# First block of a convolution and SiLU kernel: two weight units loaded ahead, first taps and some rounding moved from VectorE to ScalarE

## The chip, the cores and the metric

One core of a Trainium2 chip. The time is device microseconds of one execution of the whole program. Repeated executions of one kernel agree within some tenths of a per cent; all runs told of here are in the fast state, at a mean granted TensorE clock (the share of full speed that the throttle allowed) of 0.992 to 0.998. "VectorE", "ScalarE", "GpSimd", "SyncE" and "TensorE" are the engines; the profile calls them DVE, ACT, POOL, SP and PE, and PEld is TensorE's weight load.

## The reference

```python
# x: (8, 4096, 192); weight: (8 heads, 7 taps); w_in: (192, 2048); w_out: (2048, 192), all float32
w   = softmax(weight, axis=-1)                       # per head
y   = causal depthwise convolution of x over the sequence, 7 taps, 24 channels a head
h   = y.reshape(32768, 192) @ w_in
g   = h * sigmoid(h)                                 # SiLU
out = g @ w_out
```

The weights arrive as 64-bit floats. The kernel reads them as pairs of 32-bit words and makes float32 of them on the chip; this is the "rounding" below.

## The kernel before

The tokens are done in 32 blocks of 1024. In block 0 the plain products are computed while weights are still being made ready; blocks 1 to 31 use a scheme with fewer products that needs combined weights, and repeat a fixed plan. The change concerns block 0 and the first taps of block 1.

Each of the four units of w_in, and then of w_out, is loaded raw and rounded. A `shared` rounding gives two of its ten instructions to ScalarE; they stand in the middle, with VectorE's instructions before and behind them. Before the change the first two units of w_in are rounded so, and none of w_out:

```python
class Pinned: ...                        # keeps an engine's instructions in the program's order
vec = Pinned(nc.vector)

def rounded(dst, words, shared):         # shortened
    vec.tensor_single_scalar(ex, hi, 0x7FF * one, op=ALU.bitwise_and)
    vec.tensor_single_scalar(st, lo, 0xFF, op=ALU.bitwise_and)
    vec.tensor_scalar(ex, ex, ..., op0=ALU.max, op1=ALU.min)
    if shared:
        nc.scalar.sign(st, st)           # not pinned
        nc.scalar.activation(ex, ex, AF.Copy, bias=..., scale=8.0)
    else:
        vec.tensor_single_scalar(st, st, 1, op=ALU.min)
        vec.tensor_scalar(ex, ex, ..., op0=ALU.subtract, op1=ALU.mult)
    ...                                  # five more on VectorE; the second needs st, the fourth ex
```

The evictions of block 0 (the reads that empty TensorE's result banks) are Silu instructions on ScalarE, each of which frees one of the 8 accumulation banks. The scheduler that compiles the program may put what is not pinned in another order:

```python
def up_plain(b, j):                      # shortened: unit j, 8 banks, 24 matmuls (48 in the trace)
    hs = {(a, n, e): bank() for a, n in outs for e in range(2)}
    ...
            for e in range(2):
                nc.scalar.activation(g[:, n, e, :], hs[a, n, e], AF.Silu)

def conv(b, k, i):                       # shortened: tap i of channel third k
    if i == 0:
        pin(nc.vector.tensor_scalar(dst, src, scalar1=tap, scalar2=None, op0=ALU.mult))
    else:
        pin(nc.vector.scalar_tensor_tensor(out=dst, in0=src, scalar=tap, in1=dst, ...))

for k in range(NK):                      # head of block 0
    turn_in(0, k)                        # transpose, waits for a third of x
    for i in range(K):
        conv(0, k, i)
    spread(0, k)                         # copies to both partition halves ("dup"), SyncE's queue
    round_in(0, k)
load_in(2, nc.sync)
round_in(1)
load_in(3, nc.sync)
for j in range(NJ):                      # NJ = 4
    up_plain(0, j)
    round_in(j + 2) or round_out(j + 2 - NJ)   # and the load of w_out unit j
for j in range(2, NJ):
    round_out(j)
...                                      # transposes and taps of block 1, then down_plain(0), block 1, ...
```

Of the kernel before, what the change touches and what calls it, by code (L numbers as in the profile page):

```python
# [10 lines left out]
I32 = mybir.dt.int32  # L11
AF = mybir.ActivationFunctionType
# [5 lines left out]
def kernel(  # L18
# [24 lines left out]
    nc = tc.nc  # L43
# [3 lines left out]
    H, K = weight.shape  # L47
    NT = B * S
    DFF = moe_w_in.shape[1]
    P = 128  # L50
    R = 64
    NK = D // R
    grp = D // H
    pad = K - 1
    TB = 512
# [4 lines left out]
    NJ = NM // 2  # L60
# [10 lines left out]
    tpool = ctx.enter_context(tc.tile_pool(name="tp", bufs=3))  # L71
    gpool = ctx.enter_context(tc.tile_pool(name="gp", bufs=2 * NJ))
# [30 lines left out]
    def pin(ins):  # L103
        return tc.keep_in_program_order(ins)
# [15 lines left out]
    def load(b, ks=range(NK)):  # L120
        if b not in nats:
            nats[b] = xpool.tile([P, NK, TB // SQ, SQ], F32, tag="nat", name="nat")
        nat = nats[b]
        for k in ks:
            for i in range(P // SQ):
                c = R * k + SQ * (i % 2)
                (nc.sync if b or k or i % 2 else nc.scalar).dma_start(  # L127
                    out=nat[SQ * i : SQ * i + SQ, k, :, :],
                    in_=x_v[2 * b + i // 2][:, :, c : c + SQ],
                )  # L130
# [22 lines left out]
    WC = 2 * NK * P  # L153
# [6 lines left out]
    raws = {}  # L160

    def raw_tile(key):
        raws[key] = tpool.tile([P, 4 * TB], I32, tag="t", name="raw")[:, 0 : 2 * WC]
        return raws[key]

    def load_in(j, queue):
        raw = raw_tile(("i", j)).rearrange("p (a k c) -> p a k c", a=2, k=NK)
        for e in range(2):
            for a in range(2):
                c = 2 * P * (NM * a + 2 * j + e)  # L170
                queue.dma_start(
                    out=raw[R * e : R * e + R, a, :, :], in_=in32[:, :, c : c + 2 * P]
                )

    def load_out(q, queue):
        raw = raw_tile(("o", q)).rearrange("p (a e d) -> p a e d", a=2, e=2)
        for a in range(2):
            queue.dma_start(out=raw[:, a, :, :], in_=out32[a, q])
# [48 lines left out]
    def round_in(j, k=None):  # L227

        words = raws["i", j].rearrange("p (a k c t) -> p a k c t", a=2, k=NK, t=2)
        if k is None:  # L230
            rounded(
                wr[j].rearrange("p a k c -> p a (k c)"),
                words.rearrange("p a k c t -> p a (k c) t"),
                j < 2,
            )
        else:
            rounded(wr[j][:, :, k, :], words[:, :, k], j < 2)
        if k in (None, NK - 1):

            del raws["i", j]  # L240
            for e in range(2):
                nc.gpsimd.dma_start(
                    out=ws[j][R * e : R * e + R], in_=wr[j][R - R * e : 2 * R - R * e]
                )

    def round_out(q):
        rounded(
            wo[q].rearrange("p a e d -> p a (e d)"),
            raws.pop(("o", q)).rearrange("p (a x t) -> p a x t", a=2, t=2),
            False,  # L250
        )

    def comb(out, u, v, op):
# [24 lines left out]
        comb(a_(1, 0), a_(0, 0), a_(1, 0), ALU.subtract)  # L278

    load_in(0, nc.sync)  # L280
    load(0, (1, 2))
    load_in(1, nc.sync)


    hot = const.tile([P, NK, H], F32, name="hot")
# [38 lines left out]
    def turn_in(b, k):  # L324
        if k == 0 and b:
            xt = xts[b] = xpool.tile([P, NK, pad + TB], F32, tag="xt", name="xt")
            if b * TT % S == 0:
                nc.gpsimd.memset(xt[0:R, :, 0:pad], 0.0)
            else:
                nc.gpsimd.tensor_copy(xt[0:R, :, 0:pad], tails.pop(b))  # L330
        xt = xts[b]
        pin(
            nc.vector.transpose(  # L333
                xt[:, k, pad : pad + TB], nats[b][:, k, :, :].rearrange("p k c -> p (k c)")
            )
        )
        if k == NK - 1:
            if b:
                nc.sync.dma_start(out=xt[R:P, :, 0:pad], in_=xt[0:R, :, TB : TB + pad])
            if (b + 1) * TT % S:  # L340
                tails[b + 1] = xpool.tile([R, NK, pad], F32, tag="tail", name="tail", bufs=2)
                nc.sync.dma_start(out=tails[b + 1], in_=xt[R:P, :, TB : TB + pad])

    def conv(b, k, i):

        src = xts[b][:, k, i : i + TB]
        dst = nats[b][:, k, :, :].rearrange("p k c -> p (k c)")
        tap = taps[:, k, i : i + 1]
        if i == 0:
            pin(nc.vector.tensor_scalar(dst, src, scalar1=tap, scalar2=None, op0=ALU.mult))  # L350
        else:
            pin(
                nc.vector.scalar_tensor_tensor(  # L353
                    out=dst, in0=src, scalar=tap, in1=dst, op0=ALU.mult, op1=ALU.add
                )
            )

    def spread(b, k):

        if k == 0:  # L360
            dups[b] = xpool.tile([P, 2, NK, TB], F32, tag="dup", name="dup")
        src = nats[b][:, k, :, :].rearrange("p k c -> p (k c)")
        for n in range(2):
            for e in range(2):
                nc.sync.dma_start(
                    out=dups[b][R * e : R * e + R, n, k, :], in_=src[R * n : R * n + R, :]
                )
# [255 lines left out]
    def step(b, token):  # L623

        if token[0] == "-":
            b, token = b - 1, token[1:]
        name, arg = token.split(".") if "." in token else ("", "")
        if b < 0 or b >= NB or not name or (b, token) in did:
            return
        did.add((b, token))  # L630
        digits = [int(c) for c in arg]
        if name[0] in "PE":
            product(b, digits[0], name)
        elif name[0] in "sCg":
            if b:
                sums_h(b, name, digits[0])
        elif name == "t":
            sum_g(b, *digits)
        elif name[0] in "Mzyx":
            merge(b, name)  # L640
        elif name == "o":
            turn_out(b, *digits)
        elif b + 1 < NB:
            {"i": turn_in, "v": conv, "w": win}[name](b + 1, *digits)
            if name == "v" and digits[1] == K - 1 and (b, "down") in did:
                spread(b + 1, digits[0])
                if digits[0] == NK - 1 and b + 2 < NB:
                    load(b + 2)
# [11 lines left out]


    for k in range(NK):
        turn_in(0, k)
        for i in range(K):
            conv(0, k, i)
        spread(0, k)
        round_in(0, k)
    load_in(2, nc.sync)
    round_in(1)
    load_in(3, nc.sync)  # L670
    for j in range(NJ):
        up_plain(0, j)
        if j + 2 < NJ:
            round_in(j + 2)
            load_out(j, nc.sync)
        else:
            round_out(j + 2 - NJ)
            load_out(j, nc.sync)
        if j == 1:
            load(1)  # L680
    for j in range(2, NJ):
        round_out(j)
# [59 lines left out]
```

## Time and profile before

| part of the run before | from the trace |
|---|---|
| time, median (3 runs) | 2425.77 us (2425.73 to 2425.81) |
| span of the profiled run | 2424.1 us |
| TensorE's solid run begins with unit 2 (index 1) at | 38.20 us |
| the four units of block 0 are through at | 69.37 us |
| down products of block 0 | 41.35 us |
| up products of block 1, and of a settled block | 39.73 us, 37.97 us |

These are lines of the timeline of ScalarE in the kernel before: start, busy time, line, operation, output and input, count, and in brackets the idle time before and what ended it.

```profile
66.80 1.09 ACT L413 ACTIVATE g<-ps 128x512 f32<-128x512 f32 x2 [1.49 <-PE ps L403]
69.37 1.09 ACT L413 ACTIVATE g<-ps 128x512 f32<-128x512 f32 x2 [1.49 <-PE ps L403]
109.08 0.58 ACT L560 COPY cmb<-ps 128x512 f32<-128x512 f32 x1 [38.62 <-PE ps L547]
```

The reader is to see two things. The evictions come in twos, each released by TensorE: ScalarE keeps up and waits. And after the last one it has nothing at all to do for 38.62 us.

### The profile page before, as it was taken

What the parts mean: (1) busy time and instruction counts of PE and PEld (TensorE: products, weight loads), DVE (VectorE), ACT (ScalarE), POOL (GpSimd) and SP (SyncE); (2) the same over time, 40 slices, a digit from 0 to 9 for tenths busy, and PEclk for the clock granted to TensorE, in tenths of its full rate; (3) what the DMA queues carried; (4) which work ended last, traced back from release to release, by engine and by line L of the source; (5) the groups of instructions that cost most, each with busy time, mean ns of one, the idle gap of its engine ahead of it and who ended that gap; (6) DMA issues with size and microseconds to landing.
All of it is one profiled execution on the core that took longest, in us unless ns stands there. A gap on an engine that the chain in (4) does not pass through costs nothing.

```text
span 2424.1 us, 43022 instructions
## 1 busy us (share of the span) xinstructions
PE 2389.0 (99%) x17744; PEld 944.2 (39%) x17744; DVE 2076.5 (86%) x2827; ACT 981.7 (40%) x1845; POOL 66.4 (3%) x100
## 2 busy tenths in 40 slices
PE   6999999999999999999999999999999999999998
PEld 3344433334433334333444333443334443334432
DVE  8988888898888888888988889888889888898875
ACT  3134533345433345333454333553334543335432
POOL 3300000000000000000000000000000000000000
PEclk9999999999999999999999999999999999999999
DMA  7321222222222212221222222122222222221220
GB/s 151 73 52 32 44 44 53 41 43 40 36 53 50 43 32 42 47 53 40 41 41 39 53 48 46 31 39 50 53 40 40 38 43 53 46 43 36 36 40 14
DMA packets 452005, 111.65 MB, mean 46 GB/s; under 512 B 421792, under 2 KB 426912, under 8 KB 451808
## 3 DMA queue, kind: packets, MB, share of 16 engines
q1 hardware_dynamic: 447888, 106.63, 23.6%
q8 instruction: 139, 2.28, 0.4%
q0 software_dynamic: 608, 1.84, 0.4%
q10 hardware_dynamic: 3312, 0.42, 0.1%
q14 instruction: 58, 0.48, 0.1%
HBM read 31.49 MB, written 25.17 MB: 23 GB/s over the span
## 4 chain that ended last, share of the span: by engine, by line
PE 98%; DVE 1%; DMA 0%; SPq 0%; ACT 0%; issue 0%; POOL 0%; ACTq 0%; POOLq 0%; DVEq 0%
PE ps L439 49%; PE ps L496 46%; PE ps L547 2%; PE ps L403 1%; DVE nat L353 0%; DVE two L111 0%; SPq L127 0%; DMA nat<-in_x_dram 0%; DVE cmb L598 0%; DMA raw<-in_moe_w_in_dram 0%; DVE mh L111 0%; DVE wr L111 0%; DVE xt L333 0%; POOL out_dram L615 0%; DVE osb L608 0%
## 5 line engine op out<-in xcount | busy, mean ns | idle before, releaser
L439 PE MATMUL ps<-dup,ws 64*128 64x512 f32 x2480 | 869.1, 589 | 0.0
L496 PE MATMUL ps<-g,wo 128*32 128x512 f32 x2976 | 662.0, 593 | 0.0
L463 DVE TENSOR_TENSOR g<-u,ps 128x512 f32<-128x512 f32 x744 | 485.6, 680 | 117.6 <-PE ps L439 88.8
L439 PE MATMUL ps<-win,wr 64*128 64x512 f32 x1488 | 568.8, 589 | 0.1
L496 PE MATMUL ps<-t,wo 128*32 128x512 f32 (+1 forms) x4464 | 500.7, 450 | 0.0
L460 ACT ACTIVATE g<-g 128x512 f32<-128x512 f32 x744 | 444.7, 631 | 99.9 <-DVE g L463 99.9
L439 PEld LDWEIGHTS ps<-dup,ws 64*128 64x128 f32 x2480 | 363.8, 187 | 289.5 <-issue 273.8
L496 PE MATMUL ps<-t,wx 128*32 128x512 f32 x2976 | 453.0, 592 | 0.0
L353 DVE SCALAR_TENSOR_TENSOR nat<-xt,taps,nat 128x512 f32<-128x512 f32 x576 | 432.0, 750 | 15.1
L439 PE MATMUL ps<-dup,wr 64*128 64x512 f32 x992 | 419.3, 596 | 0.0
L454 ACT COPY u<-ps 128x512 f32<-128x512 f32 x496 | 277.5, 588 | 228.7 <-PE ps L439 225.8
L586 ACT COPY cmb<-ps 96x512 f32<-96x512 f32 x31 | 18.0, 581 | 832.2 <-PE ps L496 832.2
L480 DVE TENSOR_TENSOR t<-g 128x1024 f32<-128x1024 f32 x248 | 299.8, 1220 | 26.7 <-PE ps L496 26.7
L480 DVE TENSOR_TENSOR t<-g,t 128x1024 f32<-128x1024 f32 x248 | 303.4, 1224 | 18.3 <-PE ps L496 7.4
L439 PEld LDWEIGHTS ps<-win,wr 64*128 64x128 f32 x1488 | 234.0, 187 | 174.6 <-issue 145.7
L496 PEld LDWEIGHTS ps<-t,wo 128*32 128x32 f32 x4464 | 178.3, 110 | 222.6 <-issue 205.2
L439 PE MATMUL ps<-win,ws 64*128 64x512 f32 x496 | 241.5, 589 | 0.0
L496 PE MATMUL ps<-g,wx 128*32 128x512 f32 x1488 | 234.7, 592 | 0.0
L496 PEld LDWEIGHTS ps<-t,wx 128*32 128x32 f32 x2976 | 121.9, 110 | 278.2 <-issue 268.7
L598 DVE TENSOR_TENSOR cmb<-cmb,ps 96x512 f32<-96x512 f32 x155 | 105.7, 682 | 141.9 <-ACT u L583 139.7
L439 PEld LDWEIGHTS ps<-dup,wr 64*128 64x128 f32 x992 | 160.8, 187 | 127.2 <-issue 112.0
L496 PEld LDWEIGHTS ps<-g,wo 128*32 128x32 f32 x2976 | 168.5, 110 | 97.7 <-issue 97.7
(56 smaller groups left out, 1194.6 us busy)
## 6 DMA issues: line engine op xcount, KB each, us to landing
dup<-nat SPq DMA_DIRECT2D x384, 128.0 KB, 2.3
nat<-in_x_dram SPq DMA_DIRECT2D x382, 64.0 KB, 2.4
out_dram<-osb SPq DMA_DIRECT2D x376, 64.0 KB, 2.0
raw<-in_moe_w_in_dram SPq DMA_DIRECT2D x16, 192.0 KB, 4.8
raw<-in_moe_w_out_dram SPq DMA_DIRECT2D x8, 384.0 KB, 3.6
ws<-wr POOLq DMA_DIRECT2D x8, 192.0 KB, 4.4
xt<-xt SPq DMA_DIRECT2D x31, 4.5 KB, 1.9
tail<-xt SPq DMA_DIRECT2D x24, 4.5 KB, 1.9
```

The costliest lines, as they stand in the source:

```text
L353: nc.vector.scalar_tensor_tensor(out=dst, in0=src, scalar=tap, in1=dst, op0=ALU.mult, op1=ALU.add)
L403: nc.tensor.matmul(hs[a, n, e], rows(wr[j], e)[:, a, k, :], rows(d, e)[:, n, k, :], start=k == 0, stop=k == NK - 1,)
L439: nc.tensor.matmul(bk[b, m, bn], rows(w, half), rows(v, half), start=first, stop=True, skip_group_check=True,)
L454: pin(copy(u, bk[b, m, "1"]))
L460: pin(nc.scalar.activation(g, g, AF.Silu))
L463: pin(nc.vector.tensor_tensor(g, us.pop((b, m, i)), bk[b, m, bn], op=ALU.add))
L480: pin(nc.vector.tensor_tensor(t[i // 2][:, i % 2, :], u, v, op=ALU.subtract))
L496: nc.tensor.matmul(accs[b][i][SQ * q : SQ * q + SQ, cols], lhs[:, e, SQ * c : SQ * c + SQ], rhs[:, e, cols] if i < 5 else rhs[:, e, ts(q, ...
L547: nc.tensor.matmul(acc[k][R * n : R * n + R, :], wo[j][:, a, e, R * k : R * k + R], gs[b, j, a][:, n, e, :], start=j == 0 and a == 0 and e ...
L586: pin(nc.scalar.copy(c[0], acc[0][0:n, :]))
L598: pin(nc.vector.tensor_tensor(out_, u, v, op=ALU.add))
```

## The change

The intent: take the wait for unit 3's weights away by loading units 3 and 4 ahead into tiles that the Silu results will use later, take three first taps and part of the last roundings off VectorE, which is the chain of the first 38 us, and unit 2's load off SyncE's queue.

```diff
     def raw_tile(key):
-        raws[key] = tpool.tile([P, 4 * TB], I32, tag="t", name="raw")[:, 0 : 2 * WC]
+        pool, tag = (gpool, "g") if key in (("i", 2), ("i", 3)) else (tpool, "t")
+        raws[key] = pool.tile([P, 4 * TB], I32, tag=tag, name="raw")[:, 0 : 2 * WC]
 ...
     def round_out(q):
         rounded(..., 
-            False,
+            q >= NJ // 2,
         )
 ...
     load_in(0, nc.sync)
+    load_in(1, nc.gpsimd)
     load(0, (1, 2))
-    load_in(1, nc.sync)
 ...
-        if i == 0:
+        if i == 0 and b < 2:
+            pin(nc.scalar.activation(dst, src, AF.Copy, scale=tap))
+        elif i == 0:
             pin(nc.vector.tensor_scalar(dst, src, scalar1=tap, scalar2=None, op0=ALU.mult))
 ...
     for k in range(NK):
-        turn_in(0, k)
-        for i in range(K):
+        if k == 0:
+            turn_in(0, 0)
+            conv(0, 0, 0)
+        for i in range(1, K):
             conv(0, k, i)
         spread(0, k)
+        if k == 0:
+            load_in(2, nc.sync)
+            load_in(3, nc.sync)
+        if k < NK - 1:
+            turn_in(0, k + 1)
+            conv(0, k + 1, 0)
         round_in(0, k)
-    load_in(2, nc.sync)
     round_in(1)
-    load_in(3, nc.sync)
```

Units are counted from 0 in the code and from 1 in the text, as in the prediction: its "unit 3" is index 2. Blocks are counted from 0 in both.

## The prediction

> **What bounds the kernel now.** I began with the busy table of the page: one engine is busy for the whole span, so only idle time of that engine can be won.
>
> ```profile
> PE 2389.0 (99%) x17744; PEld 944.2 (39%) x17744; DVE 2076.5 (86%) x2827; ACT 981.7 (40%) x1845; POOL 66.4 (3%) x100
> ```
>
> The span is 2424.1 us, so TensorE lacks 35 us in all. Next came the chain of waits in order of time, to see where they lie (start, duration, what).
>
> ```profile
> 37.09 0.97 DVE wr L111
> 38.06 0.14 issue
> 38.20 31.17 PE ps L403 x144
> 69.37 41.35 PE ps L547 x192
> 110.72 20.47 PE ps L439 x88
> 131.19 0.10 issue
> 131.30 19.15 PE ps L439 x88
> 150.45 36.22 PE ps L496 x384
> 186.67 37.97 PE ps L439 x176
> ```
>
> From 38.20 us on, the chain is TensorE alone until the last merge at 2408 us. A settled block takes 36.22 + 37.97 us, 0.216 us per up matmul. Block 1 took 20.47 + 0.10 + 19.15 = 39.73 us for the same 176 matmuls: **1.76 us are lost at the passage from block 0 to block 1**. Everything else that can move lies ahead of 38.20 us. The change touches nothing in the settled loop but the first tap of block 1, so its worth is: the move of 38.20, plus what it returns of the 1.76 us, and no more.
>
> Ahead of 38.20 us the chain is VectorE. Its timeline (start, busy, line, operation, count, idle before) has no gap from the first transpose to the end of the second unit's rounding:
>
> ```profile
> 6.01 0.57 DVE L111 TENSOR_TENSOR each<-wexp,hot 128x56 f32<-128x56 f32 x3
> 6.61 0.33 DVE L111 TENSOR_REDUCE taps<-each 128x21 f32<-128x168 f32 x1
> 6.86 0.70 DVE L333 STREAM_TRANSPOSE xt<-nat 128x512 f32<-128x512 f32 x1
> 7.60 0.49 DVE L350 TENSOR_SCALAR nat<-xt,taps 128x512 f32<-128x512 f32 x1
> 8.12 4.69 DVE L353 SCALAR_TENSOR_TENSOR nat<-xt,taps,nat 128x512 f32<-128x512 f32 x6
> 12.72 0.49 DVE L111 TENSOR_SCALAR two<-raw 128x256 int32<-128x256 int32 x2
> ...
> 37.09 0.96 DVE L111 SCALAR_TENSOR_TENSOR wr<-mh,two 128x768 f32<-128x768 f32 x1
> 40.62 1.33 DVE L111 TENSOR_SCALAR two<-raw 128x768 int32<-128x768 int32 x2 [2.57 <-DMA raw<-in_moe_w_in_dram]
> ```
>
> The reader is to see three groups of transpose, seven taps and a rounding of 8.43 us each (6.86 to 15.29, to 23.74, to 32.29), then 5.77 us of rounding, and only then, at 40.62, the wait for unit 3 that the change aims at.
>
> **What the skill says.** "ScalarE: Activation LUTs", What ACT_TABLE_LOAD costs, gives 186 ns + 0.833 ns per element and some 93 ns for each pointer operand; for 512 elements with a tap as pointer 706 ns. The trace has 631 ns for a 512-element Silu from SBUF to SBUF, where the formula without pointer gives 613: it agrees. The same page, Table sets, says that cheap functions are in every set (it does not name sign). The trace has one table load at 2.39 us, and sign and copy run under it until the Silu's load at 34.95; I expect no third load. "DMA: Bandwidth & Descriptors", Issuing engines are not separate DMA queues: transfers from all queues interleave on the same 16 engines, so a second queue saves only issue time. In the trace those engines are 90% busy and more from 4 to 10 us, at some 140 to 200 GB/s. "TensorE: Matmul & The Clock Gate", Part 1, has half speed after an idle window of about 3.4 us. Here TensorE idles 3.91 us before 32.31 us, and its weight loads then come every 0.43 us instead of 0.215: it agrees.
>
> **The change, part by part.**
> (a) Units 3 and 4 ahead. This takes away the 2.57 us at 40.62. On TensorE's path it is worth nothing directly: unit 2's 48 matmuls take 48 x 0.2155 = 10.3 us from 38.20, to 48.5; the late rounding of unit 3 ended at 47.9 already. VectorE is only earlier afterwards.
> (b) First taps of block 0 on ScalarE. VectorE drops three instructions of 0.52 us start to start, 1.55 us. In return group 0 waits for the tap in series, 0.71 + 0.05 us of handing over = 0.76. For the two others ScalarE works beside the rounding, but the sign of that rounding queues behind it: it starts at 0.74 instead of 0.52 us into the rounding, which holds the OR that needs it back by about 0.2 us. Sum: 1.55 - 0.76 - 0.4 = **0.4 us gained**.
> (c) Unit 2's load through GpSimd, put ahead of the head mask in the program. GpSimd's timeline:
>
> ```profile
> 1.40 2.10 POOL L143 DMA_DIRECT2D xt<-in_x_dram  x3 [0.47 <-issue]
> 3.48 0.14 POOL L286 MEMSET hot<- 128x24 f32 x1
> 3.70 1.05 POOL L290 TENSOR_SCALAR_AFFINE_SELECT hot<-hot 64x24 f32<-64x24 f32 x4
> ```
>
> An issue there occupies the engine: 0.70 us each here, 0.55 to 0.70 for the later swaps. Four more, at an estimated 0.6 to 0.8 us, are 2.4 to 3.2 us, so the mask that was ready at 4.75 us comes at 7.2 to 8.0. VectorE needs it at 6.01 for its tap table: **1.2 to 2.0 us lost, on the path**, for both the transpose and the taps stand behind that table. The same 0.79 MB now also shares the engines with unit 1's weights and the second third of x. Those were all in by about 12 us; 0.79 MB more at some 185 GB/s is 4 us of transfer, some of it after them. I put the second third at 14 to 15 us. The new order wants it for a transpose before the rounding, at 8.5 + 6.2 = 14.7 us, where the old one first rounded and asked at 15.3. That may cost 0 to 1 us, say 0.4.
> (d) Rounding of the last two w_out units shared with ScalarE. It drops two VectorE instructions of about 0.8 us for each unit, some 1.6 us each against the old 8 us; ScalarE has nothing to do from 70.5 to 109 us. First taps of block 1: another 1 us or so. With (a) VectorE reaches block 1 some 5 us sooner. What that returns is read where TensorE's loads wait at the passage:
>
> ```profile
> 113.14 0.38 PEld L439 LDWEIGHTS ps<-dup,ws 64*128 64x128 f32 x4 [0.48 <-DMA dup<-nat]
> 120.72 0.29 PEld L439 LDWEIGHTS ps<-dup,ws 64*128 64x128 f32 x2 [0.42 <-DVE g L463]
> 130.07 0.29 PEld L439 LDWEIGHTS ps<-win,ws 64*128 64x128 f32 x2 [0.47 <-DVE g L463]
> ```
>
> All of them wait for VectorE or for a copy that VectorE's convolution released late, so I count on **1.5 of the 1.76 us**.
> Sum: + 1.6 (mask, middle) + 0.4 (x) - 0.4 (taps) - 1.5 (passage) = + 0.1 us. I allow that the scheduler may set part of GpSimd's issues behind the mask, or that they run faster than the old ones, and take 0.7 us off: 2425.77 + 0.1 - 0.7, about **2425.1 us**.
>
> **The rivals.**
> First, the plain reading of the intent: 2.57 us of wait, 1.5 of taps and 1.76 at the passage all come off the end, 2420. For it speaks that each wait is there in the trace; against it, that the first lies beside TensorE's work with 0.6 us to spare, and that one tap in three stays in series.
> Second, GpSimd or the transfers become the bound of the start: four slow issues (1 us each) put the mask at 8.8 us, a loss of 2.8, and x arrives 1 to 2 us late on top; with little returned at the passage that is 2428. For it speaks the full transfer time from 4 to 10 us; against it, that the early mask has 1.26 us of slack.
> Third, the first copies of block 0 to both halves (dup) fall behind 1.57 MB of units 3 and 4 on the same queue. At 200 GB/s these take 8 us. In the old run the first copies landed at 18.9 us and TensorE then waited anyway, so a landing at 25 still leaves 24 + 24 matmuls room before 38 us, and with less idling before the last third, so at full clock. I expect no loss, or one below 1 us.
> Fourth, ScalarE becomes a bound at 70 to 90 us: 0.85 + 0.83 us for each of two units in 38 idle us; no.
>
> **Range and chances.** The start may move by -0.6 (mask and x both in time) to +3 us, the passage returns 0.8 to 1.76 us. The ends are 2423.4 or 2422.4 with an earlier start than I can explain, and 2428.0; since both ends at once are rare, I take 2422.4 to 2427.8. Two per cent are 48.5 us; all that lies ahead of the solid TensorE work is 38.2 us, and only 7 us of matmul-free waiting stands after. So faster 0.01, slower 0.01, same 0.98.
>
> **What would show it.** In the timeline of the changed kernel: the mask's select on GpSimd after the four issues, ending at 7 to 8 us, and the tap table on VectorE waiting for it; the first tap on ScalarE at 0.7 us; an idle stretch of VectorE before the second transpose, released by x, of 0 to 1 us; TensorE's solid run beginning at 38.5 to 40 us instead of 38.20; no wait for unit 3 or 4; block 1's up matmuls in 38.0 to 38.9 us instead of 39.73; settled blocks at 74.19 us as before. The prediction is wrong downward if the mask is not held up, since then the start is at 37.7; and upward if x comes much later than 15 us, if TensorE waits for dup at 30 us, or if the settled blocks change.

## The result

The changed kernel took **2454.17 us** (median of 4 runs, 2453.81 to 2454.35) against 2425.79 us (4 runs of the kernel before, beside it): 28.4 us longer, a ratio of 1.0116 with a 95% interval of 1.0101 to 1.0131. The ratios here are taken over fast runs; they aren't quite the ratios of the medians. That is inside the 2% that were called "same", but far outside the range of 2422.4 to 2427.8.

First the chain of waits of the changed kernel after 78 us (start, duration, what). L407 is the up products of block 0, L551 its down products, L443 and L500 those of later blocks.

```profile
94.67 5.34 PE ps L407 x12
100.02 41.35 PE ps L551 x192
141.37 37.97 PE ps L443 x176
179.33 36.22 PE ps L500 x384
```

Block 0's four units are through at 100.02 us instead of 69.37. From there on nothing is slower: the down products take 41.35 us as before, and block 1's up products take 37.97 us, so the 1.76 us of the passage are all returned. The account at the end of block 1's up products: start 40.92 - 38.20 = +2.72, units 59.10 - 31.17 = +27.93, passage -1.76, in all +28.89 us. Of the span's +28.6 this leaves 0.3 us, which is gained behind the last product. So one stretch, 41 to 100 us, holds the whole loss. TensorE's timeline there:

```profile
40.92 20.87 PE L407 MATMUL ps<-dup,wr 64*128 64x512 f32 x96 [1.49 <-ACT g L417]
77.49 5.40 PE L407 MATMUL ps<-dup,wr 64*128 64x512 f32 x12 [15.70 <-ACT g L417]
84.28 5.90 PE L407 MATMUL ps<-dup,wr 64*128 64x512 f32 x24 [1.39 <-ACT g L417]
94.67 5.34 PE L407 MATMUL ps<-dup,wr 64*128 64x512 f32 x12 [4.49 <-ACT g L417]
```

Units 2 and 3 run through (96 matmuls), then TensorE waits three times, and each time what ends the wait is L417, a Silu eviction. The last unit's 48 matmuls come in pieces of 12, 24 and 12 and take from 61.8 to 100.0 us. The waits are 15.70 + 1.39 + 4.49 = 21.58 of the 27.93 us. The other 6.35 us come with them: the 48 matmuls take 16.65 us instead of 10.30, and the granted clock is 0.50 from 77 to 81 us and again from 95 to 99 us, behind the two long waits. Why are evictions late on an engine that had 38 idle us? The timeline of ScalarE (L203 and L204 are the shared rounding's sign and copy, L352 the first taps):

```profile
75.24 0.84 ACT L203 ACTIVATE two<-two 128x768 int32<-128x768 int32 x1 [22.66 <-DVE two L111]
76.11 0.84 ACT L204 ACTIVATE two<-two 128x768 int32<-128x768 int32 x1
76.86 1.07 ACT L417 ACTIVATE g<-ps 128x512 f32<-128x512 f32 x2
82.03 0.84 ACT L203 ACTIVATE two<-two 128x768 int32<-128x768 int32 x1 [4.11 <-DVE two L111]
82.89 0.84 ACT L204 ACTIVATE two<-two 128x768 int32<-128x768 int32 x1
83.64 2.04 ACT L417 ACTIVATE g<-ps 128x512 f32<-128x512 f32 x4
92.19 1.95 ACT L352 ACTIVATE nat<-xt,taps 128x512 f32<-128x512 f32 x3 [6.51 <-POOL wr L256]
94.05 3.98 ACT L417 ACTIVATE g<-ps 128x512 f32<-128x512 f32 x8
```

ScalarE is idle for 22.66 us while the eight banks of unit 3 fill (all are full when TensorE stops at 61.79 us), because the next instruction in its queue is the sign of the rounding of w_out's unit 3, and that needs VectorE. VectorE comes to that rounding at 73.79 us:

```profile
73.79 1.42 DVE L111 TENSOR_SCALAR two<-raw 128x768 int32<-128x768 int32 x2
80.58 1.42 DVE L111 TENSOR_SCALAR two<-raw 128x768 int32<-128x768 int32 x2
```

73.79 + 1.42 = 75.21, and the sign starts at 75.24; 80.58 + 1.42 = 82.00, and the second sign starts at 82.03. The order is no accident of the run: it is in the compiled queue. Runs of equal instructions of ScalarE after the table load, as compiled (the traces show the same order):

```
before:   32 Silu | 3 copies of block 0's results | ...
changed:  16 Silu | sign, copy | 2 Silu | sign, copy | 4 Silu | 3 taps of block 1 | 10 Silu | 3 copies | ...
```

The Trainium skill, "TensorE: Matmul & The Clock Gate", Part 1 (engine queue depths), says in one clause that ScalarE and VectorE are strict FIFO. The trace agrees: 22.66 us without overtaking. The wait before the taps is put down to a GpSimd instruction (L256) that was not its input. The profile names the one that came last by its inference; the taps needed block 1's transposes and the copy of its history behind them, issued at 89.79 us with a median of 1.9 us to landing. In e1, below, that copy is named.

The head, for comparison with the prediction's part (c). From the timelines of GpSimd and VectorE, changed kernel:

```profile
3.87 2.47 POOL L173 DMA_DIRECT2D raw<-in_moe_w_in_dram  x4
6.33 0.78 POOL L292 TENSOR_SCALAR_AFFINE_SELECT hot<-hot 64x24 f32<-64x24 f32 x3
7.15 0.57 DVE L111 TENSOR_TENSOR each<-wexp,hot 128x56 f32<-128x56 f32 x3 [0.94 <-POOL hot L292]
9.54 4.69 DVE L357 SCALAR_TENSOR_TENSOR nat<-xt,taps,nat 128x512 f32<-128x512 f32 x6 [0.84 <-ACT nat L352]
16.32 0.71 DVE L335 STREAM_TRANSPOSE xt<-nat 128x512 f32<-128x512 f32 x1 [2.09 <-DMA nat<-in_x_dram]
```

The four issues hold GpSimd for 2.47 us, the mask behind them (`hot`, which channel belongs to which head) makes VectorE wait 0.94 us, the serial first tap 0.84 us, and the second third of x another 2.09 us.

### The profile page after: what moved, and what is told of

Its sections match the earlier page's. It is cut to its first block, busy times and chain, and to the rows that moved or that the text cites. A ratio compares the mean times of both kernels' runs of the same rounds, so it can differ in the third digit from the quotient of the medians.

```text
span 2452.7 us, 43043 instructions
## 1 busy us (share of the span) xinstructions
PE 2394.2 (98%) x17744; PEld 940.7 (38%) x17744; DVE 2070.5 (84%) x2817; ACT 989.2 (40%) x1855; POOL 69.7 (3%) x104
## 3 DMA queue, kind: packets, MB, share of 16 engines
q8 instruction: 139, 2.28, 0.4%
## 4 chain that ended last, share of the span: by engine, by line
PE 96%; DVE 2%; SPq 1%; issue 0%; DMA 0%; ACT 0%; POOL 0%; ACTq 0%; POOLq 0%; DVEq 0%
PE ps L443 48%; PE ps L500 46%; PE ps L551 2%; DVE two L111 1%; DVE mh L111 0%; SPq L127 0%; PE ps L407 0%; DMA nat<-in_x_dram 0%; DVE cmb L602 0%; DVE nat L357 0%; DMA raw<-in_moe_w_in_dram 0%; SPq L369 0%; DVE wo L111 0%; ACT nat L352 0%; ACT g L417 0%
## 5 line engine op out<-in xcount | busy, mean ns | idle before, releaser
L443 PE MATMUL ps<-dup,ws 64*128 64x512 f32 x2480 | 869.9, 589 | 0.0
L500 PE MATMUL ps<-g,wo 128*32 128x512 f32 x2976 | 662.0, 593 | 0.0
L443 PE MATMUL ps<-win,wr 64*128 64x512 f32 x1488 | 567.7, 589 | 0.0
L500 PE MATMUL ps<-t,wo 128*32 128x512 f32 (+1 forms) x4464 | 500.7, 450 | 0.0
L443 PEld LDWEIGHTS ps<-dup,ws 64*128 64x128 f32 x2480 | 363.0, 187 | 292.0 <-issue 277.9
L500 PE MATMUL ps<-t,wx 128*32 128x512 f32 x2976 | 453.0, 592 | 0.0
L443 PE MATMUL ps<-dup,wr 64*128 64x512 f32 x992 | 419.9, 596 | 0.0
L443 PEld LDWEIGHTS ps<-win,wr 64*128 64x128 f32 x1488 | 233.4, 187 | 175.5 <-issue 147.2
L500 PEld LDWEIGHTS ps<-t,wo 128*32 128x32 f32 x4464 | 178.3, 110 | 222.6 <-issue 204.9
L443 PE MATMUL ps<-win,ws 64*128 64x512 f32 x496 | 242.2, 589 | 0.0
L500 PE MATMUL ps<-g,wx 128*32 128x512 f32 x1488 | 234.7, 592 | 0.0
L500 PEld LDWEIGHTS ps<-t,wx 128*32 128x32 f32 x2976 | 121.9, 110 | 278.2 <-issue 268.7
L443 PEld LDWEIGHTS ps<-dup,wr 64*128 64x128 f32 x992 | 160.5, 187 | 128.2 <-issue 114.3
L500 PEld LDWEIGHTS ps<-g,wo 128*32 128x32 f32 x2976 | 168.5, 110 | 97.7 <-issue 97.7
```

The source lines that it names most:

```text
L443: nc.tensor.matmul(bk[b, m, bn], rows(w, half), rows(v, half), start=first, stop=True, skip_group_check=True,)
L500: nc.tensor.matmul(accs[b][i][SQ * q : SQ * q + SQ, cols], lhs[:, e, SQ * c : SQ * c + SQ], rhs[:, e, cols] if i < 5 else rhs[:, e, ts(q, ...
```

## The experiments

Theory: an instruction of ScalarE that waits for VectorE stands in the queue ahead of evictions that are ready, and TensorE stops when its banks are full. Rivals: the moved work or the early loads slow the stretch by themselves; or block 1's taps alone do it. All experiments gave correct results. The kernel before, taken beside them, had medians of 2425.66 to 2425.74 us.

### e1: the same instructions, ScalarE's order held

```diff
-                    nc.scalar.activation(g[:, n, e, :], hs[a, n, e], AF.Silu)
+                    pin(nc.scalar.activation(g[:, n, e, :], hs[a, n, e], AF.Silu))
-            nc.scalar.sign(st, st)
-            nc.scalar.activation(ex, ex, AF.Copy, bias=..., scale=8.0)
+            pin(nc.scalar.sign(st, st))
+            pin(nc.scalar.activation(ex, ex, AF.Copy, bias=..., scale=8.0))
```

> All parts of the change kept, every instruction the same; only the ScalarE queue is held to the program's order, so that the four rounding instructions of the last two w_out units and the three first taps of block 1 stand behind all 32 Silu evictions of block 0 (in the changed kernel they stand behind the 16th, 18th and 22nd). Theory (queue order: the evictions wait behind ScalarE instructions that themselves wait for VectorE, and TensorE then finds no free bank): the 27.9 us lost between 40.92 and 100.02 go, TensorE runs its 144 matmuls from about 40.9 in 31.2 us; the late start (+2.7) and the recovered passage (-1.8) stay: about 2426.5 us. Rival 1 (the moved work itself is too slow for ScalarE, or the transfers in g tiles hold back the g tiles of unit 4): time stays near 2454, at least above 2440. Rival 2 (taps alone are to blame): the same 2426.5, so it is told apart by the next two.

Measured: **2426.2 us** (median of 4 runs, 2425.73 to 2426.36), ratio 1.0001 (0.9987 to 1.0016). The chain and ScalarE's timeline of this run:

```profile
40.71 31.17 PE ps L407 x144
71.88 41.35 PE ps L551 x192
113.23 37.97 PE ps L443 x176
```

```profile
71.88 1.09 ACT L417 ACTIVATE g<-ps 128x512 f32<-128x512 f32 x2 [1.49 <-PE ps L407]
74.95 0.84 ACT L203 ACTIVATE two<-two 128x768 int32<-128x768 int32 x1 [1.99 <-DVE two L111]
82.68 0.84 ACT L203 ACTIVATE two<-two 128x768 int32<-128x768 int32 x1 [6.01 <-DVE two L111]
92.82 1.95 ACT L352 ACTIVATE nat<-xt,taps 128x512 f32<-128x512 f32 x3 [8.42 <-DMA xt<-xt]
```

The same signs wait for VectorE, and the taps for the copy of block 1's history, at nearly the same times (74.95 against 75.24, 92.82 against 92.19), but no eviction stands behind them, and 144 matmuls take 31.17 us as before the change. Nothing was removed but the order, and 28 us went with it. This shows the cause, and excludes that the moved work, the loads ahead or the tiles they use cost that time.

### e2 and e3: sharing and taps apart

```diff
 e2: -            q >= NJ // 2,      e3: -        if i == 0 and b < 2:
     +            False,                 +        if i == 0 and b < 1:
```

> The changed kernel without the sharing of the last two w_out roundings; the taps of both blocks stay on ScalarE. In the compiled queue all 32 Silus now stand ahead of the taps. Theory (the sharing set the wrong order): about 2426.5 to 2427.5, no wait of TensorE on a Silu after 41 us. Rival (the first taps of block 1 block the queue by themselves): 2430 to 2450.

> The changed kernel with the first taps of block 1 back on VectorE; the sharing stays. The four rounding instructions still stand behind the 16th and 18th Silu. Theory: the two stretches of waiting before 84 us stay (15.7 + 1.4 us of TensorE idle, and its restarts), the third before 94.67 us goes: about 2447 us (2454 less some 7). Rival (taps to blame): 2426 to 2430.

Measured: e2 **2426.48 us** (2426.40 to 2426.72), e3 **2448.23 us** (2447.11 to 2448.94). Without the sharing the compiled queue has all 32 Silus first by itself, and the loss is gone although block 1's taps are still on ScalarE. Without the taps, TensorE's timeline keeps the first two waits and loses the third:

```profile
40.53 20.87 PE L407 MATMUL ps<-dup,wr 64*128 64x512 f32 x96 [1.48 <-ACT g L417]
77.06 4.67 PE L407 MATMUL ps<-dup,wr 64*128 64x512 f32 x12 [15.67 <-ACT g L417]
83.86 9.84 PE L407 MATMUL ps<-dup,wr 64*128 64x512 f32 x36 [2.12 <-ACT g L417]
```

The units end at 93.70 us, 6.3 earlier than in the changed kernel. So the sharing is what set the order and makes up 22 of the 28 us; the taps add the other 6, but only once the sharing has pushed evictions behind them.

### e4: the sharing alone, on the kernel before

```diff
     def round_out(q): ...
-            False,
+            q >= NJ // 2,
```

> The kernel before with nothing but the sharing of the last two w_out roundings. In the compiled queue the first pair stands behind the 18th Silu, the second behind the 20th and 21st. Theory: TensorE stops when all 8 banks are full, one pair of banks later than in the changed kernel, near 61 us, until VectorE reaches unit 3 of w_out near 73 to 75 us, and again until it reaches the fourth: 2425.8 + 15 to 20, that is 2440 to 2446. Rival (needs the early loads or the taps to do harm): 2424 to 2427.

Measured: **2444.11 us** (2444.02 to 2446.10), ratio 1.0078. The compiled queue has 18 Silus ahead of the first sign, and TensorE's timeline shows the same picture with one more pair of banks before the stop:

```profile
35.22 26.85 PE L403 MATMUL ps<-dup,wr 64*128 64x512 f32 x117
76.56 5.94 PE L403 MATMUL ps<-dup,wr 64*128 64x512 f32 x12 [14.49 <-ACT g L413]
82.87 6.63 PE L403 MATMUL ps<-dup,wr 64*128 64x512 f32 x24 [0.37 <-ACT g L413]
```

One line of the change, alone, does most of the harm.

### e5 and e6: the late start

Both are e1 with unit 2's load moved. In e5 it is where the kernel before has it; in e6 it still goes through GpSimd, but behind the mask in the program.

```diff
 e5: -    load_in(1, nc.gpsimd)          e6: -    load_in(1, nc.gpsimd)
          load(0, (1, 2))                         load(0, (1, 2))
     +    load_in(1, nc.sync)                     ... (mask)
                                             +    load_in(1, nc.gpsimd)
```

> The queue-ordered kernel of the first run with unit 2's load put back where the kernel before has it (SyncE's queue, behind all of x); everything else of the change stays. Theory (the late start of 2.5 to 2.7 us is the GpSimd load: 0.9 us of mask and some 2 us of x landing late): no wait for mask or x, TensorE's solid run from 37.6 to 38.2 us, block 1 in 38.0 us: 2425.7 - 0.3 - 1.8 = 2423.6 us. Rival (the taps on ScalarE cost the start: the serial first tap and two queued signs): start 39.0 or later, 2425 us or more.

> The queue-ordered kernel with unit 2's load still through GpSimd but put behind the mask in the program (the compiled queue lets one of its four issues slip ahead of the last two selects). Theory A (the two delays are one behind the other, as the prediction added them): mask in time, start 1 us earlier than the 40.71 of the queue-ordered kernel, 2425.2 us. Theory B (the landing of the second third of x sets the start, the mask delay only eats into that wait): the wait before the second transpose grows by what the mask gives back, start at 40.4 to 40.8, 2426.0 us.

Measured: e5 **2423.92 us** (2423.41 to 2425.09), e6 **2426.38 us** (2426.29 to 2426.56). In e5 VectorE waits for neither mask nor x, and the units are through at 68.78 us, 3.10 earlier than in e1's 71.88. These are the profiled runs; the medians differ by 2.28 us. In e6 the mask is in time, yet the solid run begins at 40.77 as in e1, since the wait for x has grown. VectorE in e6:

```profile
16.17 0.71 DVE L335 STREAM_TRANSPOSE xt<-nat 128x512 f32<-128x512 f32 x1 [3.17 <-DMA nat<-in_x_dram]
```

3.17 us instead of e1's 1.89, at the same moment (16.17 against 16.10). Theory B holds: the landing of x sets the start; the late mask only used up part of that wait. The two delays are not a sum but the larger of the two.

### e7, e8 and e9: what brings the gain

e8 is the kernel before with the early loads alone. e9 adds block 0's taps to it, and the order of transposes that goes with them. e7 is the kernel before with early loads, the sharing and block 1's taps, in held order, and the old head.

```diff
 e8:  raw_tile as in the change
      spread(0, k)
+     if k == 0:
+         load_in(2, nc.sync)
+         load_in(3, nc.sync)
      round_in(0, k)
-  load_in(2, nc.sync) ... load_in(3, nc.sync)
 e9:  the change, with: load_in(1, nc.sync) behind load(0, (1, 2)); "b < 1" for "b < 2"; False for q >= NJ // 2
 e7:  e8, with the pins of e1, q >= NJ // 2, and the first tap on ScalarE for b == 1
```

> The kernel before with the early loads of units 3 and 4 in g tiles, the shared rounding of the last two units and block 1's taps on ScalarE, all held to the program's order; the head with block 0's taps stays as before. Theory: start at 38.2 as before (early loads wait for nothing on TensorE's path), block 1 in 38.0 us: 2425.7 - 1.7 = 2424.0 us, the dup copies behind 1.57 MB of loads harmless. Rival (the early loads delay the dup copies and the start): start at 38.8 or later, 2424.7 us or more.

> The kernel before with nothing but the early loads of units 3 and 4 in g tiles. Theory: the wait of 2.57 us of VectorE goes, TensorE's start does not move (38.2), and VectorE's lead returns part of the passage's 1.76 us: block 1 in 38.2 to 39.3 us, 2424.3 to 2425.3 us. Rival (the wait was on the path): 2423.2 or less.

> The kernel before with the early loads of units 3 and 4 and the first taps of block 0 on ScalarE, and nothing else: no load through GpSimd, no sharing of the last two units, block 1's taps on VectorE, and no instruction held in order by hand (in the compiled queue all 32 Silus stand ahead by themselves). Theory (the sharing and block 1's taps return nothing that the early loads have not already returned at the passage): start and passage as in the run with unit 2's load put back, TensorE through with the units at 68.8 us, block 1 in 38.0 us, 2423.9 us within 0.5. Rival (they are worth part of the gain): 2424.5 us or more.

Measured: e7 **2424.36 us** (2423.93 to 2424.81), e8 **2424.30 us** (2424.25 to 2424.67), e9 **2424.02 us** (2423.45 to 2424.88). In all three, block 1's up products take 37.97 us. So the early loads by themselves return the whole 1.76 us, more than I expected of e8; sharing and block 1's taps, the source of the loss, are worth nothing on top. Differences of half a microsecond between e5, e7, e8 and e9 are not settled by these runs. The profiled runs of e5 and e9 have nearly the same head, but end the units at 68.78 and 69.96 us, and the busy table by stretches (29 to 33 and 33 to 36 us; granted TensorE clock is the third number from the right) shows a difference that accounts for it. First e5:

```profile
29.00:33.00 4.00, 3.96 (x11) 3.34 (x13) 3.85 (x13) 1.14 (x3) 1.10 (x2) 0.61 0.61 136
33.00:36.00 3.00, 3.00 (x16) 2.62 (x14) 2.97 (x5) 2.97 (x5) 0.44 (x2) 1.00 0.50 131
```

And e9:

```profile
29.00:33.00 4.00, 4.00 (x10) 3.23 (x12) 3.85 (x13) 1.11 (x3) 1.07 (x2) 0.50 0.61 135
33.00:36.00 3.00, 3.00 (x13) 2.45 (x11) 2.97 (x5) 2.47 (x3) 0.44 (x2) 0.73 0.50 131
```

In both runs TensorE comes out of an idle stretch at half clock. If the grant is 0.5 first and 1.0 afterwards, the means 0.61 and 0.73 put the change at 32.1 us in e5 and at 34.6 us in e9 (an estimate from these lines; the view in stretches of one microsecond bears it out: 0.50 up to 32 us and 0.94 in the next in e5, 0.50 up to 34 us and 0.70 in the next in e9). Half of these 2.5 us is 1.25, about the 1.18 us between the two ends, and the runs of e5 and of e9 spread by as much (1.7 and 1.4 us).

### e10: an instruction between the evictions that VectorE is ready for

e5 with all four w_out roundings shared. The compiled queue: 24 Silu, sign and copy, 8 Silu, then the other three pairs.

```diff
-            q >= NJ // 2,
+            True,
```

> The queue-ordered kernel with unit 2's load put back, and all four w_out roundings shared instead of two. In the compiled queue the first pair now stands behind the 24th Silu, with 8 Silus behind it. Theory (what hurts is not an instruction between the Silus but one that VectorE is not ready for: the first w_out rounding begins near 55 us, ahead of the 24th Silu near 59.5): TensorE waits for nothing, 2423.9 us within 0.7; VectorE may lose a microsecond or two to waits for ScalarE. Rival (any rounding instruction between the evictions stops TensorE): a wait of TensorE on a Silu after 55 us, 2427 us or more.

Measured: **2426.81 us** (2425.79 to 2429.81), ratio 1.0006. Half right. TensorE waits for no Silu: 176 matmuls run from 29.10 to 70.32 us without a stop, so here an instruction between evictions did no harm, with its input there (the first sign starts at 60.80, straight behind the 24th Silu). But the time is 2 to 3 us above my number. The profiled run is 2.88 us above e5's (2426.29 against 2423.41), in two parts. The units end at 70.32 us instead of 68.78, 1.54 later, and that isn't the sharing's doing, which begins at 53.36 us: half clock lasted to about 35.1 us instead of 32.1 (the same working; 0.50 up to 35 us, 0.94 in the next). The other 1.37 us are lost at the passage, because the wait turned round. VectorE:

```profile
61.67 0.99 DVE L111 SCALAR_TENSOR_TENSOR two<-raw,two 128x768 int32<-128x768 int32 x1 [5.57 <-ACT two L203]
71.97 0.96 DVE L111 SCALAR_TENSOR_TENSOR two<-raw,two 128x768 int32<-128x768 int32 x1 [2.86 <-ACT two L203]
```

VectorE now waits for ScalarE's sign, which stands behind Silus that TensorE has not yet fed: 5.57 + 2.86 = 8.4 us, not the one or two I allowed. Block 1's up products then take 39.34 us (111.67 to 151.01) instead of 37.97. What the rest of the time's spread holds (one run at 2429.81) was not looked into.

## Why the prediction was wrong

**What bounds the kernel** held: settled blocks took 74.19 us in both, and all that moved lay ahead of them.

**(a) Units 3 and 4 ahead** held. The wait vanished and the start did not move by it (e8: units through at 69.67, before 69.37). As foreseen its worth came at the passage.

**(b) Taps of block 0, 0.4 us gained**, held roughly (the taps took 0.72 us, 0.71 foreseen). From the first transpose to the end of unit 2's rounding VectorE took 31.20 us before (6.86 to 38.06) and 30.65 us in e5 (6.81 to 37.46): 0.55 us gained, with waits of 0.84 us for the serial tap and twice 0.32 us for the sign behind a tap.

**(c) Unit 2's load through GpSimd** had the mechanism right and one term too small: 1.6 + 0.4 us foreseen, 3.1 us measured in the profiled runs and 2.3 us in the medians (e1 against e5). The issues cost 2.47 us, within the estimate. The term is the landing of x: 16.1 to 16.3 us instead of "14 to 15". Since the 0.4 us was what remained of the wait for x behind the mask's delay, that landing is the whole loss: 16.10 us in e1 less 12.96 in e5, where nothing waits, is 3.14 us, and e6 shows that the mask's share is worth nothing by itself. SyncE's own eight issues of x took 10.41 us instead of 6.97; which part the shared engines have in this no run took apart.

**(d) The sharing is the step that failed**, and with it the dismissal of the fourth rival: "0.85 + 0.83 us for each of two units in 38 idle us; no." The durations were right (0.84 us each) and so was the idle time, but both were read from the old kernel's timeline, as if a free engine could take work at any time. What decides is where the new instructions stand in ScalarE's queue and what they wait for. They were compiled in behind the 16th, 18th and 22nd of 32 evictions, while their inputs came at 75 to 92 us; the evictions behind them, and then TensorE, waited. This cost 27.9 us, shown by e1. The chances rested on the same picture: they counted the idle time that TensorE already had, and the loss was new idle time in a stretch that had none. It was to be seen: in the source the evictions and the shared instructions are the only ones on ScalarE there that nothing holds in order, and the old GpSimd timeline already showed unpinned work out of the program's order (unit 1's combining at 38.70 us, ahead of unit 2's swap at 42.22).

The **1.5 of 1.76 us** at the passage was low: all of it came back, and e8 shows that the early loads alone suffice.

The **third rival** was rightly dismissed: with e8's early loads the dup copies of block 0 took a median of 4.7 us to land instead of 2.4, and TensorE's units ended 0.3 us later, at most. A sign of being wrong that the prediction named did come (TensorE waited 4.00 us for dup, until 29.68 us), but the solid run began only at 40.92 us, behind the rounding of unit 2 (to 40.77 us) and unit 1's evictions.

**Small slips of the sums**: the three groups take 8.43, 8.45 and 8.55 us, not 8.43 each; and the "7 us of matmul-free waiting" behind 38.20 us are 12, since TensorE is busy for 15.13 of the first 38.20 us and lacks 35.1 in all. Neither bears on the result.

Why the scheduler chose that order is open; no run looked into it. What the runs show is that the order changes with the sharing (e2, e4), not with the taps alone, and that holding it costs nothing measurable (e1 2426.20 us, held, against e2 2426.48, not held). The best version, e5, takes 2423.92 us, 1.7 us below the kernel before; its ratio of 0.9994 (0.9977 to 1.0011) does not set it clearly apart from it.

## What to carry to other kernels

Before moving work to an idle engine, ask not only how long it is idle but what stands behind the new instruction in that engine's queue, and when its input comes: an in-order engine passes every wait on to all that follows. Where a scheduler may reorder, look at the compiled order of the receiving engine, and hold the order of anything that frees banks or buffers for the bound engine. Two delays on different resources that meet at one instruction are worth the later one, not their sum.

## What the Trainium skill lacked or had wrong

- "ScalarE: Activation LUTs" says nothing of the order of the queue; the clause on strict FIFO stands in "TensorE: Matmul & The Clock Gate", Part 1. It deserves a place in the former: here four rounding instructions and three taps that waited in that queue (the first for 22.66 us) held back ready evictions and cost the kernel 27.9 us.
- "ScalarE: Activation LUTs" does not list sign where it tells what the function sets hold; here sign ran under the Silu's table without another load (75.24 us, between Silus).
- "DMA: Bandwidth & Descriptors" says that spreading DMAs over queues only saves issue time. It gives no figure for how long an issue occupies GpSimd (0.62 us each for 64 x 3 runs of 1 KB, 2.47 us for four), nor an example of what a load on a second queue can cost one already needed: x's second third was waited for until 16.1 us in e1, while in e5 its transpose ran at 12.96 us without a wait.
- "TensorE: Matmul & The Clock Gate", Part 1, ties the slow clock to an idle window of about 3.4 us. In e5 TensorE was idle for 2.98 us by the trace and still began at a mean granted clock of 0.61 for 4 us. The granted clock there fell at 28.7 us, 2.6 us after the end of the last matmul; in the kernel before it fell at 33.1 us, 4.7 us after such an end and 0.8 us after matmuls had begun again (estimates from the means of short stretches). Matmul ends in the trace are modelled and some records can be missing, so these gaps are rough.
